# One load that reads its source twice: the last 64 rows of Wk, Wv and W1 in a one-core attention and feed-forward kernel

## Chip, core and metric

One NeuronCore of a Trainium2 chip runs the kernel. Times are device microseconds (us) of one execution; the profile shows one profiled execution. Of the kernel's engines the text names TensorE (PE), VectorE (DVE), ScalarE (ACT), GpSimd (POOL) and SyncE (SP). SP computes nothing here: it hands out transfers to the core's 16 DMA engines, as ACT does for a few at the start.

## The reference

The input x has 2,048 tokens of 448 values in bf16. It is normalised once, and two branches read the result:

```
xn  = layernorm(x)
qkv = xn @ wqkv                      # 448 -> 3 * 448, 16 heads of 28
phi(t) = [softmax(t @ w_phi), softmax(-t @ w_phi)]      # per head, of q and of k
o   = phi(q) @ (phi(k).T @ v) / (phi(q) @ sum(phi(k)) + 1e-6)
A   = o @ wo
B   = mish(xn @ w1 + b1) @ w2        # 448 -> 1792 -> 448
out = x + A + B
```

## The kernel before

**Tiles.** The 2,048 tokens make 16 tiles of 128 (t0 to t15) and eight pairs of tiles (u0 to u7). The 448 input features are three chunks of 128 rows and a tail of 64 rows. A matmul over the tail would use half of TensorE's rows; so the tail of a weight is kept twice, in partitions 0 to 63 and in 64 to 127, and the two tiles of a pair work on the two halves side by side. That is why the last 64 rows of Wk and Wv (one source, 896 values wide), and those of W1 (1,792 wide), are loaded into both halves of column block 3.

**Stages.** For each tile the statistics (`st`), for each pair the reciprocal deviation (`rs`), the normalised pair xn (`xn`) and its transpose xnT (`xt`). A trailing d, a, p or m of a step names DVE, ACT, POOL or a DMA. Pairs 3 and 1 are transposed on TensorE (`xt3a`, `xt1d`), pairs 2, 7, 4, 5, 6 and 0 by DMA transposes that SP issues (`xt2m` is the first). Wk and Wq are multiplied with w_phi on the chip: `wtk0` to `wtk3` transpose the four row blocks of Wk on TensorE (line 556) and ACT or DVE bring them out of PSUM, `wmk` and `wmq` multiply (line 571), and `q`, `k`, `v` are the projections of a pair (line 438). `wtk3d` is the one that reads the tail of Wk, with DVE evacuating it; `v` reads the tail of Wv. Later come the features, the sum over keys, the feed-forward part (`f`, line 438 with W1 and xnT) and the output matmuls.

**What sets the order.** A table `ORDER`, written by hand, lists the steps; each engine carries out its share of them in that order. A recording layer (`Program`) notes what each step reads and writes and puts waits on semaphores in front of an instruction; each DMA has a semaphore of its own. SP's queue therefore stands in the table's order: an x load (`lx3s`), the main rows of Wk (`lkms`), the tail of Wk and Wv (`lkts`), an x load (`lx2s`), four DMA transposes of Wq (`lqT`), three x loads (`lx6s`, `lx0s`, `lx4s`), the tail of W1 (`l1ts`), the transpose `xt2m`, two chunks of W1 (`l1m2s`, `l1m0s`), the transpose `xt7m` and so on. ACT's queue has a few more loads at the start. `xt2m` waits for the x loads of tiles 0 and 15 and for POOL, which writes the normalised pair 2.

The tail's loads are made in `load_tail`, which the steps `lkts` and `l1ts` call. A reader of both halves waits for both resources, ("Wt", 0) and ("Wt", 1) for Wk and Wv, ("W1", 1) and ("W1", 2) for W1.

Of the kernel before, what the change touches and what calls it, by code (L numbers as in the profile page):

```python
# [38 lines left out]
class Program:  # L39
# [46 lines left out]
    def dma(self, eng, fn, r=(), w=(), tag=""):  # L86
        return self.op(eng, fn, r, w, dma=True, tag=tag)
# [81 lines left out]
def _kernel(es, nc, A_x, A_wqkv, A_w_phi, A_wo, B_w1, B_b1, B_w2, out):  # L169
    def sb(name, shape, dtype):  # L170
        return es.enter_context(nc.sbuf_tensor(name, shape, dtype))
# [26 lines left out]
    Wkv = sb("Wkv", [P, 4, 2 * D], BF16)  # L198
# [61 lines left out]
    op, dma = pg.op, pg.dma  # L260
# [4 lines left out]
    HALF = ((0, 64), (64, 128))  # L265
# [11 lines left out]
        dma(eng, lambda e: e.dma_start(dst[:, c, :], src[c * P:(c + 1) * P, :]), w=[(name, 0, c)], tag=f"ld{name}.{c}")  # L277

    def load_tail(eng, name, dst, src):
        for i, (lo, hi) in enumerate(HALF):  # L280
            dma(eng, lambda e, lo=lo, hi=hi: e.dma_start(dst[lo:hi, 3, :], src[384:448, :]),
                w=[("Wt", i) if name == "Wkv" else (name, 1 + i)], tag="ld" + name)

    def load_qT(g, eng):
        dma(eng, lambda e: e.dma_start_transpose(WqT[:, g, 0:D], A_wqkv[:, g * GP:g * GP + P]), w=[("WqT", g)],
# [627 lines left out]
    for eng, c in (("SP", "s"), ("ACT", "a")):  # L913
        for name, a, b in (("x0", 0, 2), ("x1", 2, 4), ("x2", 4, 6), ("x3", 6, 8), ("x4", 8, 12), ("x6", 12, 16)):
            add(f"l{name}{c}", load_x, a, b, eng)
        for i, (n, t) in enumerate((("k", Wk), ("v", Wv))):
            add(f"l{n}m{c}", load_main, eng, "W" + n, t, A_wqkv[:, (i + 1) * D:(i + 2) * D])
        add(f"lkt{c}", load_tail, eng, "Wkv", Wkv, A_wqkv[:, D:3 * D])
        for i in range(3):
            add(f"l1m{i}{c}", load_chunk, eng, "W1", W1, B_w1, i)  # L920
        add(f"l1t{c}", load_tail, eng, "W1", W1, B_w1)
        for name, fn in (("p", load_phi), ("b", load_b1), ("2", load_w2), ("o", load_wo)):
            add(f"l{name}{c}", fn, eng)
# [64 lines left out]
```

## Time and profile before

| | |
|---|---|
| median of three runs | 150.25 us (150.13 to 150.41) |
| the profiled execution: its time, its span | 150.35 us, 148.3 us |
| granted TensorE clock | 0.999 |
| DMA | 39,997 packets, 17.24 MB, mean 116 GB/s |
| queue q1 (SP's) | 16.29 MB, 52.5% of 16 engines' span |
| queue q10 (ACT's) | 0.70 MB, 1.9% |

The span runs from the first to the last instruction of the program; 2.05 us of the execution lie around it. Times within the profile count from the start of the span. PE is TensorE's matmul, PEld its weight load; SPq and ACTq are the issues of transfers, which aren't counted as busy time; "PE PS L438" is TensorE writing PSUM by line 438. The landing of a transfer counts from the start of its issue to the last update of its semaphore.

### The profile page before, as it was taken

The page shows a single profiled execution, that of the slowest core. Times are in us where ns is not written, and L with a number is a line of the kernel's source. Part 1 is how long each engine was busy: PE and PEld are TensorE (multiplying, and loading weights), DVE is VectorE, ACT ScalarE, POOL GpSimd, SP SyncE. Part 2 cuts the span into 40 slices and gives each one's busy share as a digit, 9 for nine tenths or more (in the row PEclk, how much of TensorE's full clock was granted, in tenths as well). Part 3 has the DMA queues.
Part 4 walks back from the last instruction along what each step waited for, and adds up shares of the span by engine and source line. Part 5 has one row for each costly group of instructions (what it writes and reads, how often), then busy time and mean ns, then how long its engine had stood idle before and what let it go on. Part 6 is the DMA issues. An engine that isn't in the chain of part 4 may idle for free.

```text
span 148.3 us, 3988 instructions
## 1 busy us (share of the span) xinstructions
PE 143.7 (97%) x1731; PEld 75.9 (51%) x1731; DVE 100.7 (68%) x225; ACT 72.0 (49%) x83; POOL 44.4 (30%) x65
## 2 busy tenths in 40 slices
PE   7799999999999999999999999999999999999993
PEld 2456456556555475444454445555555555554452
DVE  0888889897999803003998278896789859983042
ACT  3589889978996899578566653202000000000000
POOL 5428489899899990000000000000000000000000
PEclk9999999999999999999999999999999999999999
DMA  5999998999939989960003300031003300306513
GB/s 123 301 190 346 182 275 130 163 205 256 139 67 174 242 242 267 210 113 0 0 4 62 62 4 0 21 73 34 4 2 66 62 0 4 62 4 186 186 52 134
DMA packets 39997, 17.24 MB, mean 116 GB/s; under 512 B 33964, under 2 KB 39212, under 8 KB 39980
## 3 DMA queue, kind: packets, MB, share of 16 engines
q1 hardware_dynamic: 38800, 16.29, 52.5%
q10 hardware_dynamic: 1180, 0.70, 1.9%
q8 instruction: 13, 0.21, 0.6%
q14 instruction: 4, 0.03, 0.1%
HBM read 7.02 MB, written 1.84 MB: 60 GB/s over the span
## 4 chain that ended last, share of the span: by engine, by line
PE 89%; DMA 6%; DVE 2%; issue 0%; ACT 0%; SPq 0%
PE PS L438 47%; PE PS L843 31%; PE PS L805 3%; DMA Wkv<-in_A_wqkv_dram 3%; DMA xnT<-xn 3%; PE PS L703 2%; PE PS L629 2%; PE PS L571 1%; PE PS L821 1%; DVE stats L467 1%; PE PS L556 1%; PE PS L509 1%; DVE xnT L516 0%; ACT Eq L514 0%; DVE x_all L770 0%
## 5 line engine op out<-in xcount | busy, mean ns | idle before, releaser
L438 PE MATMUL PS<-xnT,W 64*128 64x512 bf16 x392 | 44.8, 376 | 0.0
L680 ACT ACTIVATE actT<-PS,b1T 128x1024 bf16<-128x1024 f32 x28 | 30.1, 1112 | 24.3 <-PE PS L438 24.3
L843 PE MATMUL PS<-W,actT 64*128 64x448 bf16 x392 | 39.3, 349 | 0.0
L438 PEld LDWEIGHTS PS<-xnT,W 64*128 64x128 bf16 x392 | 18.8, 94 | 20.8 <-ACT actT L680 0.5
L843 PEld LDWEIGHTS PS<-W,actT 64*128 64x128 bf16 x392 | 18.1, 94 | 18.1 <-issue 0.3
L612 POOL TENSOR_TENSOR actT<-actT,rSk 128x896 bf16<-128x896 bf16 x16 | 26.6, 1702 | 0.7 <-DVE rSk L610 0.6
L770 DVE TENSOR_TENSOR x_all<-PS,x_all 128x448 bf16<-128x448 f32 (+1 forms) x16 | 9.2, 616 | 11.3 <-PE PS L821 5.6
L718 DVE COPY Sq<-PS 128x16 f32<-128x16 f32 x32 | 4.1, 169 | 18.6 <-PE PS L703 18.5
L608 DVE TENSOR_REDUCE Sk<-actT 128x32 f32<-128x896 bf16 x16 | 16.7, 1043 | 0.0
L600 ACT ACTIVATE actT<-PS 128x896 bf16<-128x896 f32 x16 | 13.8, 950 | 1.0 <-PE PS L438 0.9
L438 PE MATMUL PS<-Wkv,xnT 64*128 64x448 bf16 x112 | 13.2, 349 | 0.0
L438 PE MATMUL PS<-Wpq,xnT 64*128 64x448 bf16 x112 | 12.5, 349 | 0.4 <-DMA xnT<-xn 0.4
L467 DVE BATCH_NORM_STATS2 stats<-x_all 128x6 f32<-128x448 bf16 x16 | 9.7, 608 | 4.1 <-DMA x_all<-in_A_x_dram 4.1
L438 PE MATMUL PS<-Wpk,xnT 64*128 64x448 bf16 x112 | 12.5, 349 | 0.0
L726 DVE TENSOR_TENSOR v_all<-v_all 128x464 f32<-128x464 f32 x16 | 10.3, 642 | 0.6
L722 DVE TENSOR_TENSOR v_all<-PS,Sq 128x464 f32<-128x464 f32 x16 | 10.3, 642 | 0.5
L729 DVE TENSOR_TENSOR xn<-v_all,rden 128x448 bf16<-128x448 f32 x16 | 10.0, 625 | 0.6
L724 DVE TENSOR_TENSOR v_all<-PS,Sq 128x464 f32<-128x464 f32 x16 | 10.1, 631 | 0.0
L661 ACT ACTIVATE actT<-PS 128x896 bf16<-128x896 f32 x10 | 8.6, 921 | 1.1 <-PE PS L438 1.1
L438 PEld LDWEIGHTS PS<-Wpq,xnT 64*128 64x128 bf16 x112 | 5.9, 94 | 5.4 <-issue 0.8
L438 PEld LDWEIGHTS PS<-Wpk,xnT 64*128 64x128 bf16 x112 | 6.0, 94 | 4.4
L438 PEld LDWEIGHTS PS<-Wkv,xnT 64*128 64x128 bf16 x112 | 6.0, 94 | 4.3
(82 smaller groups left out, 126.4 us busy)
## 6 DMA issues: line engine op xcount, KB each, us to landing
W<-in_B_w_dram SPq DMA_DIRECT2D x1, 1568.0 KB, 10.1
out_dram<-x_all SPq DMA_DIRECT2D x7, 224.0 KB, 2.1
W<-in_B_w_dram SPq DMA_DIRECT2D x3, 448.0 KB, 4.1
x_all<-in_A_x_dram SPq DMA_DIRECT2D x2, 448.0 KB, 4.9
x_all<-in_A_x_dram SPq DMA_DIRECT2D x3, 224.0 KB, 3.8
Wo<-in_A_wo_dram SPq DMA_DIRECT2D x2, 336.0 KB, 4.1
W<-in_B_w_dram SPq DMA_DIRECT2D x2, 224.0 KB, 6.4
Wkv<-in_A_wqkv_dram SPq DMA_DIRECT2D x1, 336.0 KB, 4.5
```

The lines of the kernel that those rows point to most:

```text
L438: ins = e.matmul(o, lhs(c, k), rhs(c, k), start=part == "1" and c == 0, stop=part == "2" and c == 2)
L467: op("DVE", lambda e: e.bn_stats(stats[:, t, :], x_all[:, t, :]), r=[("x", t)], w=[("st", t)], tag=f"bn{t}")
L600: op("ACT", lambda e, s=s: e.activation(E_of(u)[:, s, :, :], two(b, D), ACT.Exp, scale=1.0 if s == 0 else -1.0), r=[pb(b), pb(b + 1)], w=[ ...
L608: op("DVE", lambda e: e.tensor_reduce(Sk[u][:, s, :], Eh(), AX.X, ALU.add), r=[("E", u, s)], w=[("Sk", u, s)], tag=f"Sk{u}.{s}")
L612: op("POOL", lambda e: e.tensor_tensor(Eh(), Eh(), ap_on(rSk[u][:, s, 0:1], [[1, 2 * H], [0, DH]]), ALU.mult), r=[("E", u, s), ("rSk", u, ...
L680: op("ACT", lambda e: e.activation(actT[:, fc, q * 1024:(q + 1) * 1024], bank(b, 2), ACT.Mish, bias=b1T[:, fc:fc + 1]), r=[("b1T",), pb(b) ...
L722: op("DVE", lambda e: e.tensor_tensor(tv(t1[i]), num(0), sx(1), ALU.mult), r=[pb(b), pb(b + 1), ("Sq", i, 1)], w=[("t1", i)], tag=f"ta{t}")
L724: op("DVE", lambda e: e.tensor_tensor(tv(t2), num(1), sx(0), ALU.mult), r=[pb(b), pb(b + 1), ("Sq", i, 0)], w=[("t2",)], tag=f"tb{t}")
L726: op("DVE", lambda e: e.tensor_tensor(t1[i], t1[i], t2, ALU.add), r=[("t1", i), ("t2",)], w=[("t1", i)], tag=f"tc{t}")
L729: op("DVE", lambda e: e.tensor_tensor(o_sb[(t // 2) % 2][:, t % 2, :].rearrange("p (h d) -> p h d", d=DH), t1[i][:, :, 0:DH], ap_on(rden[i ...
L770: op("DVE", lambda e: e.tensor_tensor(x_all[:, t, 0:n], bank(b)[:, 0:n], x_all[:, t, 0:n], ALU.add), r=[pb(b), ("x", t)], w=[("out", t)], ...
L843: ins = e.matmul(bank(places[par][0])[:, 0:D], l, r, start=fresh[par], stop=places[par][2] and i >= len(todo) - 2)
```

## The change

`load_tail` issues one DMA instead of two. Its destination is column block 3 of all 128 partitions. Its source is the same 64 rows, with a leading dimension of 2 and a step of 0 put in front, so that the rows are read twice. The one DMA is noted as writer of both halves. The table `ORDER` is the same; line numbers behind the edit move by two.

```diff
     def load_tail(eng, name, dst, src):
-        for i, (lo, hi) in enumerate(HALF):
-            dma(eng, lambda e, lo=lo, hi=hi: e.dma_start(dst[lo:hi, 3, :], src[384:448, :]),
-                w=[("Wt", i) if name == "Wkv" else (name, 1 + i)], tag="ld" + name)
+        def twice():
+            rows = src[384:448, :]
+            return bass.AP(tensor=rows.tensor, offset=rows.offset, ap=[[0, 2]] + [list(d) for d in rows.ap])
+        dma(eng, lambda e: e.dma_start(dst[:, 3, :], twice()),
+            w=[("Wt", i) if name == "Wkv" else (name, 1 + i) for i in range(2)], tag="ld" + name)
```

On SP's queue, from the first load to the transpose `xt2m`, the program before has these rows (the destination's shape behind the names; the rows with Wkv and W at L281 are the tails):

```order
L273 DMA Wkv<-in_A_wqkv_dram 128x3x448
L281 DMA Wkv<-in_A_wqkv_dram 64x896 x2
L270 DMA x_all<-in_A_x_dram 128x896
L285 DMA_TRANSPOSE WqT<-in_A_wqkv_dram 128x448 x4
L270 DMA x_all<-in_A_x_dram 128x1792
...
L281 DMA W<-in_B_w_dram 64x1792 x2
L521 DMA_TRANSPOSE xnT<-xn 128x7x128 [waits dma_9,dma_10,done_POOL]
```

Now the same stretch of the queue has these:

```order
L273 DMA Wkv<-in_A_wqkv_dram 128x3x448
L283 DMA Wkv<-in_A_wqkv_dram 128x1x896
L270 DMA x_all<-in_A_x_dram 128x896
L287 DMA_TRANSPOSE WqT<-in_A_wqkv_dram 128x448 x4
L270 DMA x_all<-in_A_x_dram 128x1792
...
L283 DMA W<-in_B_w_dram 128x1x1792
L523 DMA_TRANSPOSE xnT<-xn 128x7x128 [waits dma_8,dma_9,done_POOL]
```

Each pair of issues has become one, at the same place; nothing has passed anything else, and the two semaphores that `xt2m` waits for are those of the same two x loads, with numbers one lower. On TensorE the rows differ only in the number of semaphores waited for: the transposes of `wtk3d` wait for one DMA instead of two.

## The prediction

> **What bounds the kernel now.** I read the page's busy times first, then the waits of TensorE, then the chain that ended last, and last the transfers of the first 20 us. The share of each engine:
>
> ```profile
> PE 143.7 (97%) x1731; PEld 75.9 (51%) x1731; DVE 100.7 (68%) x225; ACT 72.0 (49%) x83; POOL 44.4 (30%) x65
> ```
>
> TensorE is busy for 143.7 of 148.3 us. All that it ever waited for:
>
> ```profile
> PE PS L376 <- PEq L973: 0.8, 1, 0.8
> PE PS L556 <- DMA Wkv<-in_A_wqkv_dram: 0.4, 1, 0.4
> PE PS L438 <- DMA xnT<-xn: 0.4, 1, 0.4
> PE PS L571 <- ACT Eq L514: 0.3, 1, 0.3
> ```
>
> Two of the four waits are for transfers, 0.4 us each. So nothing done to the loads can win more than 0.8 us, while a load that comes late stops an engine that has no idle time in which to make it good. The chain that ended last (start, length, what) shows where loads are nearly late:
>
> ```profile
> 7.48 0.39 PE PS L509 x7
> 7.87 0.38 PE PS L556 x4
> ...
> 11.56 0.50 PE PS L571 x8
> ...
> 14.22 4.29 DMA xnT<-xn
> 18.51 0.14 issue
> 18.64 34.54 PE PS L438 x350
> ```
>
> The four L556 matmuls at 7.87 transpose the last 64 rows of Wk (step wtk3d); they wait for the tail load. At 18.64 TensorE needs the transpose of xn pair 2 (step xt2m), which took 4.29 us to land; from there it runs on without a gap. The span is 148.3 us of a run of 150.35; the median of the runs shown is 150.25, so a shift of the profile applies to either. A measurement of this kernel can tell about 0.2% (0.3 us) from no change.
>
> **The SP queue in that stretch.** Its timeline (start, length of the issue, what):
>
> ```profile
> 1.73 1.19 SPq L281 DMA_DIRECT2D Wkv<-in_A_wqkv_dram  x2
> 2.97 0.59 SPq L270 DMA_DIRECT2D x_all<-in_A_x_dram  x1
> 3.60 5.12 SPq L285 DMA_TRANSPOSE WqT<-in_A_wqkv_dram  x4
> 8.77 1.53 SPq L270 DMA_DIRECT2D x_all<-in_A_x_dram  x3
> 10.34 1.12 SPq L281 DMA_DIRECT2D W<-in_B_w_dram  x2
> 14.22 1.26 SPq L521 DMA_TRANSPOSE xnT<-xn  x1
> 15.53 1.50 SPq L277 DMA_DIRECT2D W<-in_B_w_dram  x2
> ```
>
> And the landing (last number, us from issue) of four single issues: the second Wk/Wv tail, the last WqT transpose, the last x load, the second W1 tail:
>
> ```profile
> Wkv<-in_A_wqkv_dram SPq DMA_DIRECT2D x1, 112.0 KB, 5.4
> WqT<-in_A_wqkv_dram SPq DMA_TRANSPOSE x1, 3.1
> x_all<-in_A_x_dram SPq DMA_DIRECT2D x1, 448.0 KB, 5.9
> W<-in_B_w_dram SPq DMA_DIRECT2D x1, 224.0 KB, 6.9
> ```
>
> Issued at 2.33 (1.73 and half of 1.19), 7.44 (3.60 and three quarters of 5.12), 9.79 (8.77 and two thirds of 1.53) and 10.90, they land at 7.73, 10.5, 15.7 and 17.8; xt2m, issued at 14.22, lands at 18.51. Landings follow the order of issue: what stands behind a slow load on SP's queue lands behind it.
>
> **What the change removes.** Two issues. Each costs SP this much (min/median/max ns):
>
> ```profile
> L281 SPq DMA_DIRECT2D Wkv<-in_A_wqkv_dram x2: 562/576/590, 1.7 to 2.3; - x2
> L281 SPq DMA_DIRECT2D W<-in_B_w_dram x2: 482/536/591, 10.3 to 10.9; - x2
> ```
>
> So what follows on SP is issued up to 0.58 us earlier, and after the W1 tail up to 1.1 us. The bytes are the same: each half of the partitions still gets its own copy. This gain counts only if the transfers themselves stay as quick.
>
> **What the change adds.** The source of the new load is read as 2 x 64 x row, with a leading count of 2 and a step of zero. The price hangs on how many of the 16 DMA engines carry such a load. No row of this trace shows a leading count of 2, so I bound it: 16 engines, as for the loads with 64 or 128 rows in front, or 2. One row bears on it, that of the only load whose leading count is not a multiple of 16 (b1: 14 rows), beside another small load of the same queue:
>
> ```profile
> Wraw<-in_A_w_phi_dram ACTq DMA_DIRECT2D x1, 24.5 KB, 3.0
> b_rows<-in_B_b_dram ACTq DMA_DIRECT2D x1, 3.5 KB
> ```
>
> It alone has no landing time: its completion does not read like that of a load spread over 16. That is a hint that the engines used go by the leading count, so I take 2. [...]
>
> What one engine carries, from two windows, 11.1 to 12.9 us (loads alone) and 2 to 6 us (both queues together):
>
> ```profile
> q1 hardware_dynamic: 285, 0.68, 96.3%
> ...
> q1 hardware_dynamic: 648, 0.73, 62.6%
> q10 hardware_dynamic: 784, 0.39, 42.0%
> ```
>
> The first gives 0.68 MB / (0.963 x 16 x 1.8 us) = 24.5 KB per us and engine; the second 1.12 MB / (1.046 x 16 x 4 us) = 16.7, with all engines pulling at HBM. With two engines active the first is the nearer.
>
> Step by step on the two engines:
> - Wk/Wv tail: 64 rows of 1,792 B each instead of 8, so 56 more, 100 KB: 4.1 us (6.0 at the slow rate). It lands at 7.73 + 4.1 = 11.8. TensorE, done at 7.87 with L509, waits 4.0 us there. DVE stands behind it at the evacuation of wtk3d, and behind that the statistics of x.
> - lx2s and the four WqT transposes stand behind it on SP: the last lands at 10.5 + 4.1 = 14.6. TensorE needs them 3.7 us after wtk3d (L571 at 11.56 in the chain), so now at 11.8 + 3.7 = 15.5: hidden, by 0.9 us.
> - The three x loads (10 tiles of 112 KB; the 448 KB above are four) are issued before the two engines reach them. 1,120 KB / 16 = 71.7 KB per engine: 2.9 us, to 17.5. That is only 1.8 later than 15.7. Before, 5.2 us lay between the last WqT and the last x, issue time among it, with the engines partly idle:
>
> ```profile
> 9.30:10.40 1.10, 1.10 (x13) 0.46 (x11) 1.07 (x4) 0.88 (x3) 0.77 (x2) 1.00 0.64 82
> ```
>
> (the last three numbers: granted clock 1.00, DMA share 0.64, 82 GB/s).
> - W1 tail: 64 rows of 3,584 B, 229 KB per engine: 9.4 us (13.7 at the slow rate), to 26.9. W1 itself is wanted only by the feed-forward part, some 20 us after xt2m:
>
> ```profile
> 39.83 1.04 PE L438 MATMUL PS<-xnT,W 64*128 64x512 bf16 x8
> ```
>
> - xt2m waits on SP for the x loads and for POOL's xn pair 2. That pair hangs on DVE's statistics, which stand behind wtk3d, so xt2m is issued 4.0 us later than before, at 18.2: in time, but queued behind the W1 tail. It lands 18.51 - 17.8 = 0.7 after it: 27.7, with rounding.
> - TensorE does its 10.4 us of work between wtk3d and xt2m (7.87 to 18.64 less the wait of 0.40) from 11.8 to 22.2 and waits 5.5 us, until 27.7. After that the order is as before, with TensorE as the bound: everything is late by 27.7 - 18.5 = 9.2 us. The first wait of 4.0 lies within it and is not added.
>
> What is late next: the two W1 chunks and xt7m follow xt2m at their old distance, and TensorE reaches xt7m's pair at its old distance too, so nothing more is added.
>
> **TensorE's clock** is the last term. The twelve warm-up matmuls at the start, all of them and the first ten:
>
> ```profile
> 0.85 4.65 PE L376 MATMUL PS<-const-bfloat16-1.0 128*128 128x512 bf16 x12 [0.85 <-PEq L973]
> ...
> 0.85 4.21 PE L376 MATMUL PS<-const-bfloat16-1.0 128*128 128x512 bf16 x10 [0.85 <-PEq L973]
> ```
>
> Ten take 0.42 us each, the last two 0.22 each: coming from idle, TensorE loses 10 x 0.20 = 2.0 us before it is at full speed. Whether a wait in the middle costs this again, no row shows, since after the start it never waits over 0.4 us. Bounds 0 and 2.0. Losses after the wait for wtk3d are hidden in the one for xt2m and shorten it (5.5 to about 3.5 us), so only one after xt2m counts, and I take 0.8. [...]
>
> The sum: 150.35 + 9.2 + 0.8 = 160.35, 160.3 us.
>
> **The rivals.**
> - B, two engines and the clock lost in full after xt2m's wait: 9.2 + 2.0 = 11.2, so 161.5; with the slow rate on the Wk/Wv tail too (1.9 more), 163.5. For it: a wait of 3 to 5 us is far longer than any here. Against: TensorE comes to that wait later if it loses its clock in the first, and then waits less.
> - C, faster: all 16 engines carry the new load. Then only the saved issues are left: the loads behind land 0.6 to 1.1 us earlier, xt2m's wait of 0.4 goes, and wtk3d gains nothing, for TensorE is busy until 7.87. 150.35 - 0.4 = 149.9. For it: every 64- and 128-row load here is spread. Against: the row of b1. It decides from the point at which the W1 tail lands before 17.8.
> - D, hidden in part: two engines, but xt2m passes the W1 tail. Then the Wk/Wv tail's 4.0 us is left, less the 0.4 wait: 150.35 + 3.6 = 154.0. Against: landings follow the issue order.
>
> **How the numbers follow.** Forecast 0.58, B 0.25, C 0.12, D 0.05. The range holds the forecast and B: its low end is the forecast without the clock term and with the two long loads a tenth quicker and a microsecond of other delays gone (150.35 + 9.2 - 1.35 - 1.0 = 157.2), its high end B with the slow rate on that tail, 163.5. C and D are left out, 0.17. Slower by over 0.2% is the forecast, B and D: 0.88. C's 0.4 us is near what can be told: 0.07 faster, 0.05 no change.
>
> **What would show it.** In the changed profile the two loads should land about 10 and 17 us after issue, where the halves took 4.8 to 6.9 (the Wk/Wv tail near 11.8, the W1 tail near 27); DMA share should sink far below 0.9 between 18 and 26 us; TensorE should have two new waits, about 4.0 us at L556 for Wkv and 3.5 to 5.5 us at L438 for xnT; from there on all should run as before, 9 us later, with the clock seen in whether L438's starts lie further apart after the wait. The prediction is wrong if the loads land as before, if xt2m lands before the W1 tail, or if new waits show after 30 us.

## The result, and the profile after

The changed kernel takes 160.85 us (median of six runs, 159.55 to 162.64) against 150.49 us for the kernel before, run beside it: 1.0658 times as long (95% interval 1.0601 to 1.0716), so 10 us slower. The ratio is taken over the fast runs alone (one of the six, 162.64 us, is slow), so it is not the quotient of the two medians. The forecast was 160.3 us. The profiled execution took 159.55 us, with a span of 157.8 us against 148.3: 9.5 us more.

All that TensorE waited for in the changed kernel (us in total, times, longest):

```profile
PE PS L440 <- DMA xnT<-xn: 3.6, 1, 3.6
PE PS L558 <- DMA Wkv<-in_A_wqkv_dram: 3.4, 1, 3.4
PE PS L378 <- PEq L975: 0.8, 1, 0.8
PE PS L573 <- ACT Eq L516: 0.3, 1, 0.3
```

The two waits of 0.4 us for transfers have become waits of 3.4 and 3.6 us, at the same two places: the transposes of the last Wk rows (line 558 now) and the first matmul that needs xt2m. There is no third. The chain that ended last shows what each of them hung on:

```profile
1.74 9.35 DMA Wkv<-in_A_wqkv_dram
11.13 0.44 PE PS L558 x4
...
17.53 9.07 DMA xnT<-xn
26.74 35.96 PE PS L440 x350
```

The one load of the Wk/Wv tail, issued at 1.74, lands at 11.1 (the second of the two before: 7.7). The transpose xt2m, issued at 17.53, lands at 26.6 (before: 18.5), that is 8.1 later. The stretch behind it, the same 350 matmuls, takes 35.96 us instead of 34.54: 1.42 more. 8.1 + 1.4 is the 9.5 us of the span.

How many engines carried the load is seen where nothing else was left to carry. The first row is the stretch in which TensorE waits for the Wk tail, the second and third lie within the time of the W1 tail; the last three numbers are granted clock, DMA share and GB/s:

```profile
8.00:11.00 3.00, 0.00 (x0) 0.00 (x0) 0.00 (x0) 0.76 (x1) 0.00 (x0) 1.00 0.13 51
20.00:24.00 4.00, 3.14 (x34) 1.41 (x30) 3.84 (x14) 3.37 (x5) 2.42 (x5) 1.00 0.13 54
19.50:21.00 1.50, 1.50 (x20) 0.78 (x16) 1.43 (x5) 1.17 (x2) 0.93 (x2) 1.00 0.88 53
12.60:16.00 3.40, 3.40 (x21) 1.25 (x19) 2.72 (x11) 1.30 (x3) 2.41 (x6) 0.50 1.00 327
26.20:29.60 3.40, 2.86 (x16) 1.39 (x18) 3.26 (x11) 0.02 (x1) 3.05 (x7) 0.51 1.08 337
```

A DMA share of 0.13 is 2/16: two engines, with 51 GB/s, 25 each, and fourteen that move next to nothing. The second row has it again: 0.13, 54 GB/s. In the third row two engines move 53 GB/s; its share of 0.88 can't be the share of two engines. A packet counts from its start to its end, and three packets of the transpose xt2m that start between 19.5 and 19.6 us end only at 25.5. So the bytes tell more than the share. The last two rows are for TensorE's two waits: its granted clock is 0.50 from 1.5 us after the end of the first, and from 0.5 us before the end of the second, for 3.4 us each time.

The queue of SP in the stretch of the prediction:

```profile
1.74 0.69 SPq L283 DMA_DIRECT2D Wkv<-in_A_wqkv_dram  x1
2.48 0.42 SPq L270 DMA_DIRECT2D x_all<-in_A_x_dram  x1
2.95 8.39 SPq L287 DMA_TRANSPOSE WqT<-in_A_wqkv_dram  x4
11.39 1.53 SPq L270 DMA_DIRECT2D x_all<-in_A_x_dram  x3
12.96 0.57 SPq L283 DMA_DIRECT2D W<-in_B_w_dram  x1
17.53 1.44 SPq L523 DMA_TRANSPOSE xnT<-xn  x1
```

One issue costs 0.69 and 0.57 us where two cost 1.19 and 1.12. The page gives no landing time for either load, as for that of b1 before:

```profile
Wkv<-in_A_wqkv_dram SPq DMA_DIRECT2D x1, 224.0 KB
```

The semaphore updates in the trace say why. In the kernel before, each of the four tail loads, with 64 rows in front, has 16 of them when it has landed. The changed load of Wk and Wv has one about 1 us after its issue and then only two, at 11.08 and 11.09 us; that of W1 has one, and then two at 25.60 and 25.64. The load of b1 with its 14 rows has one early and fourteen later. So in these traces the updates behind the first agree with the two engines of the DMA share. The x load behind the changed Wk/Wv load (`lx2s`) has fourteen of its 16 updates by 7.2 us and the other two at 11.66: its share on the two engines stood behind the tail.

The four WqT transposes now take 8.39 us to issue instead of 5.12: SP itself was held up.

### The profile page after: what moved, and what is told of

It reads as the page before. It is cut to its first block, busy times and chain, and to the rows that moved or that the text cites. A ratio compares the mean times of both kernels' runs of the same rounds, so it can differ in the third digit from the quotient of the medians.

```text
span 157.8 us, 3984 instructions
## 1 busy us (share of the span) xinstructions
PE 147.1 (93%) x1731; PEld 77.1 (49%) x1731; DVE 101.5 (64%) x225; ACT 72.1 (46%) x83; POOL 44.4 (28%) x65
## 4 chain that ended last, share of the span: by engine, by line
PE 81%; DMA 12%; DVE 2%; POOL 2%; SPq 1%; issue 1%; DVEq 0%
PE PS L440 43%; PE PS L845 29%; DMA Wkv<-in_A_wqkv_dram 6%; DMA xnT<-xn 6%; PE PS L807 3%; PE PS L705 2%; PE PS L631 2%; POOL xn L498 1%; DVE stats L469 1%; PE PS L823 1%; POOL rstd L478 0%; DVE x_all L772 0%; DVE mv L470 0%; PE PS L558 0%; DVE Eq L518 0%
## 5 line engine op out<-in xcount | busy, mean ns | idle before, releaser
L845 PEld LDWEIGHTS PS<-W,actT 64*128 64x128 bf16 x392 | 18.7, 94 | 17.5 <-issue 0.3
L440 PE MATMUL PS<-Wpq,xnT 64*128 64x448 bf16 x112 | 13.9, 380 | 3.6 <-DMA xnT<-xn 3.6
L720 DVE COPY Sq<-PS 128x16 f32<-128x16 f32 x32 | 4.0, 168 | 18.6 <-PE PS L705 18.5
L440 PE MATMUL PS<-Wkv,xnT 64*128 64x448 bf16 x112 | 14.3, 374 | 0.0
L440 PE MATMUL PS<-Wpk,xnT 64*128 64x448 bf16 x112 | 13.0, 359 | 0.0
```

The costliest lines, as they stand in the source:

```text
L440: ins = e.matmul(o, lhs(c, k), rhs(c, k), start=part == "1" and c == 0, stop=part == "2" and c == 2)
L845: ins = e.matmul(bank(places[par][0])[:, 0:D], l, r, start=fresh[par], stop=places[par][2] and i >= len(todo) - 2)
```

## The experiments

The theory: the leading count of a load's source decides how many of the 16 DMA engines carry it; two engines take 64 rows each, and the transposes of xn stand behind them. The rivals: reading the same rows again is what is slow; each load costs for itself; the clock plays no part; another queue or another place in the order would hide it. Each experiment was timed beside the kernel before on the same chip. The first four ran together (the kernel before: 150.73 us), the next four together (150.44), the last two together (150.54).

### Two groups of rows, without reading twice

```diff
+        def in_two():
+            rows = src[384:448, :]
+            (step, n), cols = rows.ap
+            return bass.AP(tensor=rows.tensor, offset=rows.offset, ap=[[step * (n // 2 - 1), 2], [step, n // 2], list(cols)])
         for i, (lo, hi) in enumerate(HALF):
-            dma(eng, lambda e, lo=lo, hi=hi: e.dma_start(dst[lo:hi, 3, :], src[384:448, :]),
+            dma(eng, lambda e, lo=lo, hi=hi: e.dma_start(dst[lo:hi, 3, :], in_two()),
```

> The kernel before, two loads for each tail, but each reads its 64 rows as 2 x 32 with a step of 31 rows between the two groups, so that the leading count is 2 and only one row is read twice (the last 64 weight rows are shifted by one in the upper group: the output is not the reference's, the work is the same). Theory (the leading count sets how many DMA engines carry a load): both loads of a tail go over the same two engines, 64 rows on each as in the changed kernel, so 160.8 us (159.5 to 162.5), with the two waits of TensorE of 3 to 5 us. Rival (what is slow is reading the same rows again through a step of zero): no more than before, 150.5 us.

Measured: 162.56 us, 1.0761 times the kernel before (1.0679 to 1.0843). Two loads with 64 rows each, as before, only one row of each read again, and the whole cost is there. The stretch before the Wk tail lands reads as in the changed kernel:

```profile
8.50:11.00 2.50, 0.00 (x0) 0.00 (x0) 0.00 (x0) 0.20 (x1) 0.00 (x0) 0.99 0.13 50
```

Two engines, 50 GB/s. The step of zero is not needed for the cost; the leading 2 is enough. The 0.06 us over the expectation's upper end go with the clock: in the profiled execution it is 0.50 for 6.8 us at each of the two waits, twice as long as in the changed kernel, and the 350 matmuls behind xt2m take 37.46 us instead of 35.96:

```profile
28.00:34.83 6.83, 5.95 (x33) 2.84 (x35) 3.56 (x13) 3.11 (x4) 6.26 (x14) 0.50 1.23 197
```

```profile
28.88 37.46 PE PS L442 x350
```

The two of its four runs with a mean clock of 0.968 took 161.6 us, within the expectation; the two with 0.957 and 0.958 took 163.5 and 163.6.

### Each row twice in a row: leading count 64

```diff
-            return bass.AP(tensor=rows.tensor, offset=rows.offset, ap=[[0, 2]] + [list(d) for d in rows.ap])
+            row, cols = rows.ap
+            return bass.AP(tensor=rows.tensor, offset=rows.offset, ap=[list(row), [0, 2], list(cols)])
```

> The changed kernel, one load for each tail, its source read as 64 x 2 with the step of zero inside: each row is read twice in a row, and the leading count is 64 (row r goes to partitions 2r and 2r+1, so the output is not the reference's, the bytes and issues are those of the changed kernel). Theory: all 16 engines carry it, and only the saved issues are left: 150.1 us (149.7 to 150.6), the tails landing near 7.5 and 17. Rival (reading rows again is slow, or a source of three dimensions is): about 160 us as in the changed kernel.

Measured: 149.41 us, 0.9910 times the kernel before (0.9879 to 0.9941). One load, the same bytes, each row read twice, three dimensions: with 64 in front it is not only harmless, it is faster than before. The waits of TensorE for transfers:

```profile
PE PS L559 <- DMA Wkv<-in_A_wqkv_dram: 0.3, 1, 0.3
...
PE PS L441 <- DMA Wkv<-in_A_wqkv_dram: 0.2, 1, 0.2
```

The wait for xnT is gone. So neither reading again nor the third dimension costs anything here. This is also what the change would have done had all engines carried its load (rival C of the prediction). The gain is 0.6 us by the spans (147.7 against 148.3), 1.3 us by the medians; the prediction's 0.4, and the 149.7 to 150.6 expected here, were too cautious.

### Four copies: leading count 4

```diff
-            return bass.AP(tensor=rows.tensor, offset=rows.offset, ap=[[0, 2]] + [list(d) for d in rows.ap])
+            (step, n), cols = rows.ap
+            return bass.AP(tensor=rows.tensor, offset=rows.offset, ap=[[0, 4], [step, n // 2], list(cols)])
```

> The changed kernel with the source read as 4 x 32, step of zero outside: 32 rows four times, leading count 4 (wrong rows in part of the tail, the same bytes). Theory: four engines, 32 rows on each: the Wk/Wv tail 24 rows later per engine (43 KB at 27 KB per us, 1.6 us), the W1 tail about 4.3 us of carrying instead of 8.5, so it lands near 20.6 and the first transpose of xn by DMA near 21.4, 2.9 later than before: 153.3 us, up to 154.5 if TensorE's clock falls once. Rival (reading rows again is slow): four readings are no quicker than two, 160 us or more.

Measured: 153.61 us, 1.0169 (1.0115 to 1.0222). A window ahead of the landing of the Wk tail, and the chain:

```profile
8.10:9.10 1.00, 0.00 (x0) 0.00 (x0) 0.09 (x1) 0.98 (x2) 0.00 (x0) 1.00 0.26 94
```

```profile
1.72 7.44 DMA Wkv<-in_A_wqkv_dram
...
15.60 6.79 DMA xnT<-xn
```

The share is 0.26, four of sixteen, with 94 GB/s. The Wk/Wv tail lands at 9.2 and xt2m at 22.4, between the kernel before (7.7 and 18.5) and the change (11.1 and 26.6). xt2m is 1.0 later than expected; the time agrees with the expectation all the same. The changed loads have two semaphore updates at their end here for a leading count of 2, four for 4 and 16 for 64: the engines at work are 2, 4 and all.

### W1 alone, and Wk and Wv alone

W1's tail as changed, the other in two loads:

```diff
+        if name == "Wkv":
+            for i, (lo, hi) in enumerate(HALF):
+                dma(eng, lambda e, lo=lo, hi=hi: e.dma_start(dst[lo:hi, 3, :], src[384:448, :]),
+                    w=[("Wt", i) if name == "Wkv" else (name, 1 + i)], tag="ld" + name)
+            return
```

> The change for W1 alone; Wk and Wv as before. Theory (the first wait is hidden in the second): the x loads land at 15.7 as before, the W1 tail about 8.7 later, near 24.5, the transpose behind it near 25.3, 6.8 later than before; TensorE waits some 7 us there, so its clock falls and 1.4 to 2 us more are lost: 158.7 us (157.5 to 159.8), most of the change's cost. Rival (each load costs for itself, by its rows): two thirds of the 10.4 us, 157.3 us, and the rest from Wk and Wv.

And the other way round:

```diff
-        if name == "Wkv":
+        if name == "W1":
```

> The change for Wk and Wv alone; the W1 tail in two loads as before. Theory: TensorE waits 3.4 us for the Wk tail and loses 1.6 us by its clock behind it; the transpose xt2m, issued near 17.5, lands near 20.7, before TensorE comes to it near 23: 150.4 + 4.5 = 154.9 us (153.2 where the clock does not fall, up to 155.3). With the W1 part alone that is more than the whole change costs, since in the whole the first wait lies within the second. Rival (each load costs for itself, the two parts adding up to the 10.4 us of the change): about 2 to 3.4 us, 152.4 to 153.8.

Measured: W1 alone 157.84 us, 1.0465 (1.0421 to 1.0509); Wk and Wv alone 155.39 us, 1.0333 (1.0306 to 1.0360). The first result alone lies between the two expected figures, and within the theory's range; its xt2m lands at 24.1 (expected near 25.3). The second is 0.1 above the theory's range and far above the rival's. Together they decide: 7.1 and 5.0 us make 12.1, and the whole change costs 10.4 by its medians. The parts cost more apart than together, because in the whole change the first wait lies within the second. The waits for transfers, W1 alone (first fence) and Wk and Wv alone:

```profile
PE PS L445 <- DMA xnT<-xn: 5.8, 1, 5.8
PE PS L563 <- DMA Wkv<-in_A_wqkv_dram: 0.9, 1, 0.9
```

```profile
PE PS L563 <- DMA Wkv<-in_A_wqkv_dram: 3.3, 1, 3.3
```

With W1 alone TensorE comes early to xt2m and stands for 5.8 us; with Wk and Wv alone it comes so late that xt2m has landed.

### TensorE kept busy in the two waits

The steps `z14` are 14 idle matmuls each, as in the warm-up. The table of the changed kernel, at the two places:

```diff
-wtk3d lqT1
+z14 wtk3d lqT1
...
-v12d q21
+v12d z14 q21
```

> The changed kernel with 14 idle matmuls (as in the warm-up at the start) put on TensorE ahead of the step that waits for the Wk tail and 14 ahead of the one that waits for xt2m; nothing else is changed. Theory (part of the cost is TensorE's clock, which falls in these waits): granted clock back at 0.99 or more, the runs close together, and 1.4 us or more gained: 158.6 us (158.0 to 159.2). Rival (the landing of xt2m is all): as the changed kernel, 160.8 us, whatever the clock.

Measured: 159.12 us, 1.0596 (1.0549 to 1.0643), 0.5 over the expected figure and within its range. The clock is 0.999 over the profiled execution, and its chain has the stretch behind xt2m in this row:

```profile
26.91 34.54 PE PS L440 x350
```

34.54 us, to the digit what the 350 matmuls took before, and 35.96 in the changed kernel. xt2m lands no earlier. So 1.42 us of the change's cost in its profiled execution are TensorE's clock, and the rest is xt2m. The two kernels were not measured beside each other and their intervals overlap, so the gain in the medians (1.7 us) is the weaker evidence. The runs did not come close together as expected: they took 158.37 to 159.92 us with a mean clock of 0.989 to 1.000. So not all of the spread between runs is the clock.

### The W1 tail on ACT's queue

```diff
-wmq0a xn2p l1ts xt1d
+wmq0a xn2p l1ta xt1d
```

> The changed kernel with the load of the W1 tail issued by ACT at the same place of the order instead of SP. It still goes over two engines. Theory (the transpose is late because it stands behind the W1 tail in SP's queue on these engines, and two queues take turns): xt2m lands near 22, before TensorE comes to it near 23: about 154.9 us (154.0 to 156.5), the cost of the Wk/Wv tail alone. Rival (a full engine holds up the handing out of transfers on both queues): xt2m lands as late as in the changed kernel or later, 160.8 us or more.

Measured: 162.78 us, 1.0830 (1.0797 to 1.0863). Both expectations had the mechanism wrong. ACT's issue stands in ACT's order behind work for TensorE and came only at 18.05, after xt2m's. The waits of TensorE in the timeline:

```profile
25.32 2.07 PE L440 MATMUL PS<-Wpq,xnT 64*128 64x448 bf16 x20 [1.12 <-DMA xnT<-xn]
...
34.56 1.68 PE L440 MATMUL PS<-Wkv,xnT 64*128 64x448 bf16 x8 [4.53 <-DMA xnT<-xn]
```

xt2m lands near 25.2, 1.4 before that of the changed kernel, but 7.3 us after its issue, though the W1 load was handed out after it and on the other queue; the next transpose, xt7m, costs 4.5 us more. Of xt2m's 16 semaphore updates fourteen come by 21.0 us and the last two at 24.7 and 25.2. So a load on ACT's queue slowed a transfer on SP's here as well: two of the 16 updates came 3.7 and 4.2 us behind the others, which fits two engines that both queues share. SP's issue of xt2m was not held (1.26 us), so the rival's reason does not hold for it, though the rival's time does; an issue further on was (5.51 us for the first transpose EqT, 1.31 in the kernel before).

### The W1 tail behind xt2m, in the kernel before

```diff
-wmq0a xn2p l1ts xt1d
+wmq0a xn2p xt1d
...
-q11 xt2m st8d
+q11 xt2m l1ts st8d
```

> The kernel before with the two loads of the W1 tail moved one place back on SP, behind the transpose xt2m. Theory (xt2m's last 0.4 us of waiting is its place behind the W1 tail in the queue): xt2m lands near 17.7, TensorE's wait of 0.4 goes, 150.0 us (149.8 to 150.3). Rival (xt2m's time to land does not hang on what stands ahead of it): 150.4, no change.

Measured: 152.03 us, 1.0103 (1.0076 to 1.0130): slower. The theory was right about xt2m, which lands 3.0 us after its issue at 14.67 instead of 4.3, and wrong about what is late next. The chain has it:

```profile
18.78 5.98 DMA xnT<-xn
24.89 5.26 PE PS L438 x53
```

This is xt7m: 5.98 us to land instead of 3.0. The W1 tail and the two chunks of W1 now stand right ahead of it on SP, issued from 16.02 to 18.34, and TensorE waits 1.6 us there. In the place that it had, the tail was under way while SP waited for xn pair 2 (11.5 to 14.2 us).

### The second half by another queue

Here the loads keep 64 rows in front and SP still saves an issue:

```diff
-            dma(eng, lambda e, lo=lo, hi=hi: e.dma_start(dst[lo:hi, 3, :], src[384:448, :]),
+            dma(eng if i == 0 or name == "W1" else "ACT", lambda e, lo=lo, hi=hi: e.dma_start(dst[lo:hi, 3, :], src[384:448, :]),
```

> The kernel before; of the two loads of the Wk/Wv tail the second is issued by ACT, right behind its x load, instead of SP. All loads keep 64 rows in front. Theory (what the changed kernel meant to win is SP's issue time of 0.58 us ahead of lx2s and all that follows, and loads over 16 engines give it): xt2m lands 0.5 or more earlier, near 17.9, TensorE's wait of 0.4 there goes: 149.5 to 150.0 us, 0.3 to 0.7 under before, as in the run with each row read twice. Rival (the gain of that run came from one load instead of two on the DMA engines, not from SP's time): no gain, 150.4.

For the next, the W1 tail too:

```diff
-            dma(eng if i == 0 or name == "W1" else "ACT", lambda e, lo=lo, hi=hi: e.dma_start(dst[lo:hi, 3, :], src[384:448, :]),
+            dma(eng if i == 0 else "ACT", lambda e, lo=lo, hi=hi: e.dma_start(dst[lo:hi, 3, :], src[384:448, :]),
```

> As the run before, and of the W1 tail the second load too is issued by ACT, between its evacuations of Wpq. Theory (by then xt2m's landing hangs on the transfers, not on SP's issue): nothing more, 149.5 to 150.0 us; ACT's 0.5 us of issue lies in its waits for TensorE. Rival (ACT's issue holds up the evacuations that TensorE waits for): 0.3 to 0.5 us back, 150.2 us or more.

Measured, 12 runs each: 150.11 us, 0.9964 (0.9935 to 0.9993), and 149.79 us, 0.9940 (0.9912 to 0.9969). Both beat the kernel before, the second by 0.6%; between the two there is no telling. The first is 0.1 above its expected range, but the gain of 0.4 us is the expected one, for the kernel before took 150.54 beside it. Its xt2m lands at 17.5. In the first, TensorE has no wait for a transfer left:

```profile
PE PS L376 <- PEq L973: 0.8, 1, 0.8
PE PS L438 <- ACT Eq L661: 0.3, 1, 0.3
PE PS L571 <- ACT Eq L514: 0.2, 1, 0.2
```

xt2m's wait is gone, as expected, and a new one of 0.3 us on ACT further on gives part of it back; the span of this execution is 148.4 us, as before, so its profile shows the move of the waits and only the medians show the gain. In the profiled execution of the second, the main load of Wk landed late (a wait of 1.4 us, span 148.7); it is not typical of the median.

## Why the prediction was right

The sign, the place and the mechanism were right, and the time within 0.6 us, that last in part by luck. By its own steps:

- **Two engines.** Right, and shown: a DMA share of 0.13 with 51 GB/s in the changed kernel, 0.26 with 94 GB/s for a leading count of 4, none of the cost for 64, and two, four and 16 semaphore updates at the loads' ends. The hint from the 14-row load of b1 was a good one: the two changed loads have no landing time on the page either. It has fourteen updates behind its first, they have two each.
- **The Wk/Wv tail, forecast at 11.8.** It landed at 11.1; the first wait was 3.4 instead of 4.0. The rate was as taken (25 GB/s per engine, against 24.5 KB per us), so the start was too late: the prediction adds the 4.1 us for 56 more rows to the end of the old load, that is to the last of its 16 engines. In the kernel before, that load's 16 updates lie between 6.49 and 7.77 us. 100 KB at 25 GB/s, counted back from 11.1, begin at 7.1, within these. Whether the two engines were early ones was not tried.
- **WqT hidden.** Right: no wait for it appeared.
- **xt2m, forecast at 27.7.** It landed at 26.6, the step that was most off: 8.1 us late instead of 9.2. The last x load shows how much stood before the W1 tail; it was issued at 12.48:

```profile
x_all<-in_A_x_dram SPq DMA_DIRECT2D x1, 448.0 KB, 4.7
```

So it landed at 17.2, forecast 17.5. The W1 tail landed at 25.6, forecast 26.9: 8.4 us behind the x load and not 9.4, for 54 GB/s on two engines is 27 each and not 24.5. xt2m came 1.0 behind the tail, a little more than the 0.7 of the forecast. The issue time of 18.2 came out as 17.53. The sign that the prediction names, a DMA share far below 0.9, is met from 20 to 24 us (0.13); right before, the stalled packets hide it.
- **Nothing late behind it.** Right: no wait for a transfer after 27 us. How near that was is seen in the eighth experiment, where xt7m became late by 1.6 us.
- **The clock, 0.8.** It was 1.42 us in the profiled execution, shown by the run with idle matmuls. The clock fell at both waits, of 3.4 and 3.6 us, to 0.50 for 3.4 us each time; the run with Wk and Wv alone, whose one long wait is 3.3 us, has a mean clock of 0.976 in its profiled execution. The argument that the first loss shortens the second wait was right (3.6 instead of 5.5), but not that this would save the clock.
- **The sum** is right because two errors cancel, and that is luck: 1.1 too much for xt2m, 0.6 too little for the clock. The median is above the profiled execution's 159.55 us, and the clock goes with it: the runs with a mean granted clock of 0.978 took 159.6 and 160.1 us, those with 0.967 or 0.968 took 160.8 to 161.3. In the changed kernel's trace the clock is at half twice, for 3.41 us each; in that of the first experiment for 6.83 us at a wait, twice as long. One stretch of 3.41 us takes about 1.1% off the mean of a run of 158 us (an estimate from these two numbers), so 0.978 is two stretches, as in the profiled execution, and 0.968 would be three. So the run of the median probably lost a third, and 0.8 was further off for it than the profile shows.

Of the rivals, B was nearly met on the clock; its slow rate was not. C needs all 16 engines, and the run with 64 in front shows that it would then have been right and even too small. By the medians (1.3 us) that run also won more than the 0.8 us that the prediction put as the most that any change of the loads can win; by the spans (0.6 us) it did not. D (xt2m passes the W1 tail) did not come about; with the load on the other queue it did in part, and cost more.

## What to carry to other kernels

Look at the leading count of a load's source, not only at its bytes and its destination: here a repeat put in front as 2 x 64 halved the issues and left fourteen of sixteen DMA engines without a share in the load (DMA share 0.13), and what stood behind it in the queue landed later (xt2m by 8.1 us). Where a repeat is wanted, keep a large count in front, if the layout allows it (the run with 64 in front puts the rows into other partitions than this kernel needs, so it shows the time only), or keep two loads and spread their issue over two queues. Before a load is moved, ask which later transfer will then stand behind it, and count a long stop of TensorE as longer than it is, for the clock: in the profiled executions here with a wait of 3.3 to 5.8 us the mean granted clock was 0.957 to 0.978, in those without a wait over 2.8 us 0.999 or 1.000.

## What was not expected of the hardware

While two engines carried the tails, the other fourteen came to a stop as well: the DMA share was 0.13 from 8 to 11 us and from 20 to 24. SP's four WqT issues took 8.39 us instead of 5.12. ACT's load of Wv's main rows, issued on its own queue at 2.5 us and with 16 semaphore updates, landed this long after its issue in the changed kernel:

```profile
Wkv<-in_A_wqkv_dram ACTq DMA_DIRECT2D x1, 336.0 KB, 9.2
```

Before it was 5.2. Its bytes were not late by that much: between 8 and 11 us ACT's queue has next to nothing left to move (packets, MB, share):

```profile
q10 hardware_dynamic: 5, 0.00, 0.3%
```

Two of the load's 16 semaphore updates come at 8.6 us, the other fourteen only at 11.6, after the Wk/Wv tail had landed at 11.1. In between, something had begun and did not end: 26 packets of 256 bytes on SP's queue, which only its transposes have, start between 6.8 and 7.8 us and all end at 11.5 to 11.6. (The trace does not name the engine of a packet. That they are on the fourteen is the author's reading: the tail, still moving at 51 GB/s until 11 us, was issued ahead of the transposes.) The same is seen at xt2m: 17 such packets start between 19.2 and 19.6 us and all end at 25.5, when the W1 tail is done. The two chunks of W1 issued behind xt2m seem to move nothing until then, for 54 GB/s over the 8.4 us is the tail alone. So in this trace packets of a DMA transpose that had begun ended only at the landing of the tail ahead of it, 0.4 us behind it at WqT and 0.1 us ahead of it at xt2m, and the loads behind waited too; that the transpose waited for the two engines is the reading that fits. That the late updates of ACT's load waited for these packets fits the times and was not tried. They are not on the chain that ended last.
